# Where k and v of a batch are kept, and when k^T v and the sums of w_in are made, in a one-core attention and feed-forward kernel

## The chip, the cores and the metric

The kernel runs on one core of one Trainium2 chip. The metric is the device time of one execution in microseconds (us); lower is better. One execution was also taken by the hardware profiler, and all readings of engines, waits and transfers come from that one.

## The reference

A linear attention without softmax is followed by a normalisation, and its result goes through a feed-forward block whose activation is a squared ReLU with a scale and a bias. All is float32 in the kernel (weights may come in as wider words and are converted on the chip).

```
# q, k, v: (8 batches, 8 heads, 576 positions, 64); w_in: (512, 2048); w_out: (2048, 512)
kv  = einsum('bhsd,bhse->bhde', k, v)
out = einsum('bhsd,bhde->bhse', q, kv)
out = out / sqrt(mean(out*out, axis=-1) + 1e-6) * g_norm
x   = out.transpose(0, 2, 1, 3).reshape(4608, 512)
h   = x @ w_in
r   = maximum(h, 0)
y   = (s * (r * r) + b) @ w_out
```

## The kernel before, in words

**Chunks and units.** The 4608 rows of x are cut into 36 chunks of 128 rows, and four chunks make a unit: nine units, u = 0 to 8. Unit by unit the kernel multiplies 512 rows by w_in (the part called mm1), squares, and multiplies by w_out (mm2), while the attention of the next unit's four chunks is worked in between. Unit 0 also converts the weights and forms the sums of blocks of w_out, and works its first product plainly.

**Fewer products by sums.** From unit 1 on the products use Strassen's scheme in the variant of Winograd: seven products of half-size blocks instead of eight, with sums of blocks of both operands. For mm1 the names x1, x6, y7, x5, x3, y4 are steps of one of four slices s of w_in's columns; slices come in pairs (d = 0: slices 0 and 1, d = 1: slices 2 and 3), and in the code a is the first slice of the pair and b the second. One of the seven products is itself made by a second level of the scheme, for both slices of a pair together: `mm1_twice`, m[1], m[2], m[6], m[7], m[5], m[34]. The sums of w_in's blocks that these need are made once, by VectorE in unit 1: `sums_w_in(s)` (lines 245 to 259: four operations of 128x512 for a slice) and `sums_w12(s)` (lines 267 to 273: four operations of 128x128 for a slice). `sums_w(s, *more)` (line 1274) calls both.

**The steps that matter here.** m[1] adds its product from PSUM into the hidden tile by an addition on VectorE (`to`, line 663, shown as L231 in the profile, since `add` is a helper), and m[6] accumulates into the bank that this addition has read. Step x6 ends with a copy of its PSUM bank into a tile r2 by ScalarE (ACT; `keep`, line 606). r2 has one buffer, so b's r2 is written only when a's has been read, by the addition in y4 (line 644). x5 accumulates into the bank that r2 was copied from.

**k^T v.** `kv_product(b)` makes, for a batch, the 64x64 product of every head, on quarters of TensorE's array, into two PSUM tiles, and ACT copies them into the block-diagonal bd_kv. Batches 0 and 1 are made in unit 0. Batches 2 to 7 fall due in units 1 to 6 (`kv_due`, line 1238), and are made in two halves of four heads (`kv_half`, line 1280): the first after a["x6"] of d = 0, the second after a["x3"] of d = 1. Both halves come through one buffer of their own (`late["kv"]`, line 1107), so a half is loaded when the half before it has been multiplied: four DMAs of 288 KB for a half, two of k and two of v. The very first of them is issued when unit 0 is done (line 1357).

**The ring of w_out's operands.** The blocks of w_out and their sums lie in DRAM and come in through seven buffers of 128x1024 floats (`ringp`, line 1103). `queue_w2` (line 709) is the list of all these loads in the order of their use, and `pump(k)` issues the next k of them. Unit 0 ends with pump(7), and mm2 calls pump(2) after every other step or so, so that seven loads stay ahead.

**The queues.** The order of each engine's work is that of the code[...]. All loads and stores of this part are issued by SyncE (SP), in the code's order: out's stores, the ring's loads, k and v, and q. `loads(u, i)` (line 1240) loads q of the next unit's chunks in two parts: i = 0 at the unit's start, i = 1 after the place of the first kv half. VectorE turns q (line 418): the first two chunks of the next unit at `second["turns"]` in d = 1, the other two during mm2.

Of the kernel before, what the change touches and what calls it, by code (L numbers as in the profile page):

```python
# [9 lines left out]
FP32 = mybir.dt.float32  # L10
# [6 lines left out]
def kernel(  # L17
# [40 lines left out]
    nc = tc.nc  # L58
    P = 128
    B, H, S, D = q.shape  # L60
    DM = H * D
    DF = moe_w_in.shape[1]
    HB = P // 2
    R = S // HB
    JC = S // 32
    NP = H // 2
# [4 lines left out]
    U = CH // 4  # L71
    NS = FC // 4
    HN = DM // 2
# [10 lines left out]
    ps_t = ctx.enter_context(tc.tile_pool(name="ps_t", bufs=2, space=bass.MemoryType.PSUM))  # L84
# [10 lines left out]
    kv_in, q_in, w_raw = {}, {}, {}  # L95

    def load_kv(b, i, pool, queues=(nc.sync, nc.sync), **kw):

        t = pool.tile([P, 4 * R * D], U32, name="kv_sb", **kw)
        kv_in[b, i] = t.bitcast(FP32).rearrange("p (m l j d) -> p m l j d", m=2, l=2, j=R)  # L100
        for m, src in enumerate((k, v)):
            for r, queue in enumerate(queues):
                h = NP * r + 2 * i
                queue.dma_start(  # L104
                    out=kv_in[b, i][r * HB : r * HB + HB, m].rearrange("p l j d -> p l (j d)"),
                    in_=src[b, h : h + 2].rearrange("h (p j) d -> p h (j d)", j=R),
                )

    def parts(c):
# [229 lines left out]
    for h in range(H):  # L339
        e = D // KC  # L340
        nc.gpsimd.dma_start(
            out=g_col[h * e : h * e + e, :], in_=g_norm.rearrange("(e c) -> e c", c=KC)
# [19 lines left out]
    def warm(n):  # L362

        ps = ps_f.tile([P, 2, TB], FP32, name="warm_ps", tag="z", bufs=1)
        for _ in range(n):
            matmul(ps[:, 0, :P], ident, ident, True, True)

    kv_ps = {}

    def kv_product(b, halves=(0, 1)):  # L370


        if halves[0] == 0:
            kv_ps[b] = [ps_t.tile([P, 2, D], FP32, name="kv_ps", tag="t") for _ in range(2)]
        ps = kv_ps[b]
        for i in halves:
            if b == 0:
                warm((18, 7)[i])
            kv = kv_in.pop((b, i))
            for j in range(R):  # L380
                for l in range(2):
                    for r in range(2):
                        rows = slice(r * HB, r * HB + HB)
                        nc.tensor.matmul(  # L384
                            ps[r][l * HB : l * HB + HB, i, :],
                            lhsT=kv[rows, 0, l, j, :],
                            rhs=kv[rows, 1, l, j, :],
                            start=(j == 0),
                            stop=(j == R - 1),
                        )  # L390
        if halves[-1] == 0:
            return
        for r in range(2):
            for l in range(2):
                ls = slice(l * HB, l * HB + HB)
                to = bd_kv[b % 2][ls, 2 * r : 2 * r + 2, ls].rearrange("p i (c e) -> p i c e", c=KC)
                src = ps[r][ls].rearrange("p i (e c) -> p i c e", c=KC)
                if b == 0 and l == 1:
                    nc.vector.tensor_copy(out=to, in_=src)
                else:  # L400
                    nc.scalar.copy(to, src)
# [296 lines left out]

    ring = {}
    ORDER = (1, 2, 6, 7, 5, 3, 4)
    late = {}

    def twice(u, i):
        return u > 1 and i in TWICE

    queue_w2 = [
        (u, i, n) for u in range(1, U) for i in ORDER for n in range(4 if twice(u, i) else 2)  # L710
    ]

    def pump(k):

        for u, i, n in queue_w2[:k]:
            t = late["ring"].tile([P, 4 * HN], FP32, name="w2_sb", tag="w2")
            if twice(u, i):
                t = t.rearrange("p (m f n) -> p m f n", m=2, n=P)
                k2 = min(2, 7 - 2 * n)
                nc.sync.dma_start(out=t[:, :k2], in_=w3_dram[i][:, 2 * n : 2 * n + k2])  # L720
            else:
                t = t.rearrange("p (f n) -> p f n", n=HN)
                nc.sync.dma_start(out=t, in_=w2_dram[i][:, 4 * n : 4 * n + 4])
            ring[u, i, n] = t
        del queue_w2[:k]
# [375 lines left out]
    def tc_late():  # L1101
        convp.release()
        late["ring"] = ctx.enter_context(tc.tile_pool(name="ringp", bufs=7, side="right"))
        late["sub"] = ctx.enter_context(tc.tile_pool(name="subp", bufs=5, side="right"))
        late["tmp"] = ctx.enter_context(tc.tile_pool(name="tmpp", bufs=4, side="right"))
        late["w"] = ctx.enter_context(tc.tile_pool(name="latep", bufs=1, side="right"))
        late["kv"] = ctx.enter_context(tc.tile_pool(name="kvp", bufs=1, side="right"))

    blocks = [i for s in range(NS) for i in (2 * s, NU + 2 * s)]
    blocks += [FC + 2 * s for s in range(2 * NS)]  # L1110
# [39 lines left out]
    for i in range(2):  # L1150
        load_kv(0, i, kv0p, two, tag="kv")
# [81 lines left out]
            }  # L1233
        return side

    kv_due = {(b // 2 * R + b % 2 * 4) // 4 - 1: b for b in range(2, B)}

    def loads(u, i):  # L1240
        if u + 1 < U:
            load_q(4 * u + 4 + 2 * i)
# [15 lines left out]
    for u in range(U):  # L1258
        if u > 0:
            loads(u, 0)  # L1260
        steps = [mm1(u, s) for s in range(NS)] if u > 0 else []

        def x3(a):
            for name in ("x3", "x3_square", "x3_s1", "x3_s3"):
                a[name]()

        def y4(a):
            for name in ("y4", "y4_square"):
                a[name]()

        side = side_of(u)
        second = mm2(u, steps[-1], side) if u > 1 else mm2(u)

        def sums_w(s, *more):
            for sums in sums_w_in(s):
                sums()
            for s in more:
                sums_w12(s)

        def kv_half(i):  # L1280
            kv_product(kv_due[u], (i,))
            if i == 0:
                load_kv(kv_due[u], 1, late["kv"], tag="kv")
            elif u + 1 in kv_due:
                load_kv(kv_due[u + 1], 0, late["kv"], tag="kv")

        if u == 0:
            first_unit()
        for d in range(NS // 2 if u > 0 else 0):
            a, b = steps[2 * d : 2 * d + 2]  # L1290
            m = mm1_twice(u, d)
            if u == 1 and d == 0:
                x21_sums(1)
                sums_w(1, 0, 1)
            a["x1"]()
            if d:
                x3(steps[2 * d - 1])
                y4(steps[2 * d - 1])
            b["x1"]()
            m[1]()  # L1300
            a["x6"]()
            if d == 0:
                if u in kv_due:
                    kv_half(0)
                loads(u, 1)
            elif u > 1:
                second["turns"]()
            m[2]()
            m[6]()
            a["y7"]()  # L1310
            m[7]()
            m[5]()
            a["x5"]()
            if d == 0 and u == 1:
                sums_w(2)
            m[34]()
            a["x3"]()
            if d and u in kv_due:
                kv_half(1)
            for name in ("x3_square", "x3_s1", "x3_s3"):  # L1320
                a[name]()
            y4(a)
            if u == 1 and d == 0:
                sums_w(3, 2, 3)
            b["x6"]()
            b["y7"]()
            if d and u > 1:
                second["sums"]()
            b["x5"]()
        if u > 1:  # L1330
            second["rest"]()
            continue
        for n, slot in enumerate(second):
            slot()
            if u == 0:
                if n == 1:
                    for i in range(2):
                        load_kv(1, i, convp, tag="raw", bufs=3)
                    store_w2(1)
                    loads(0, 0)  # L1340
                    loads(0, 1)
                    store_w2(5)
                elif n == 2:
                    t2 = convp.tile([P, 4 * R * D], FP32, name="w_t2", tag="raw", bufs=3)
                    W2_AT[6] = t2[:, : FC // 2 * HN].rearrange("p (f n) -> p f n", n=HN)
                    for i in range(14, 16):
                        more(i)
                    sub_w_out(6, 3, 5)
                    store_w2(3, 2, 6)
            if n == 0 and u > 0:  # L1350
                x3(steps[-1])
                y4(steps[-1])
            for step in side.get(n, []):
                step()
        if u == 0:
            tc_late()
            load_kv(kv_due[1], 0, late["kv"], tag="kv")
            pump(7)


# [28 lines left out]
```

## Time and profile before

| | |
|---|---|
| Median of the runs | 961.72 us (960.79 to 964.14, 3 runs) |
| The profiled execution | 961.81 us, of which 960.0 us is the span from the first instruction to the last |
| Mean granted clock of TensorE | 0.996 of full speed |
| TensorE busy with matmuls | 940.3 us |
| VectorE busy | 641.4 us |
| ScalarE busy | 194.8 us |
| DMA | 151.11 MB moved, mean 157 GB/s |
| k and v loads by SP | 60 DMAs of 288 KB, median 4.3 us (k) and 5.5 us (v) from issue to landing |

PE is TensorE's matmuls, PEld its weight loads, DVE is VectorE, ACT is ScalarE, SPq is SyncE's queue of DMA issues. In the lines that are shown below, a line of the timeline gives the start in us, the time in us, the engine, the line of the code, the operation, what it writes and reads with sizes, how many records are merged, and in brackets how long the engine stood idle before it and for whom. A line of the waits gives who waited for whom, the total, how often, and the longest. A line of a stretch gives its limits and length, the busy time of PE, PEld, DVE, ACT and POOL with the number of records, the granted clock, the busy share of the DMA engines, and GB/s. A matmul of float32 is recorded as two instructions: a kv product of 72 matmuls has 144 records.

### The profile page before, as it was taken

The numbers are of one execution on the slowest core, as the hardware profiler recorded it, in microseconds if no ns is written. First come the engines' busy times: TensorE is split into PE (matmuls) and PEld (weight loads), VectorE is DVE, ScalarE is ACT, GpSimd is POOL, SyncE is SP. The second block draws the span as 40 slices with busy tenths as digits, with TensorE's granted clock in tenths as the row PEclk, the third lists the DMA queues.
The fourth block names the chain that finished last, engine by engine and source line by source line (L and its number), as shares of the span: only waits on it lengthen the run. The fifth ranks groups of instructions, "written<-read, shape, count | busy, mean of one in ns | idle before, by whom it ended". The sixth has DMA issues, their size and how long they took to land.

```text
span 960.0 us, 17707 instructions
## 1 busy us (share of the span) xinstructions
PE 940.3 (98%) x7294; PEld 844.4 (88%) x7294; DVE 641.4 (67%) x1212; ACT 194.8 (20%) x366; POOL 6.7 (1%) x18
## 2 busy tenths in 40 slices
PE   7999997999999999999999999999999999999997
PEld 7888886788889998899889998989899989998997
DVE  2789765776566864787468746884678567865673
ACT  3783130111111121102121211111111111121100
POOL 2000000000000000000000000000000000000000
PEclk9999998999999999999999999999999999999999
DMA  9689737368644647255626563556415541642063
GB/s 244 209 304 248 245 84 228 74 196 259 206 111 103 206 147 181 64 177 192 171 36 185 186 181 77 158 183 196 89 54 190 184 103 34 209 153 89 17 224 100
DMA packets 131711, 151.11 MB, mean 157 GB/s; under 512 B 76592, under 2 KB 89136, under 8 KB 131504
## 3 DMA queue, kind: packets, MB, share of 16 engines
q1 hardware_dynamic: 128528, 148.22, 53.3%
q10 hardware_dynamic: 2784, 1.77, 0.8%
q8 instruction: 57, 0.93, 0.4%
q14 instruction: 22, 0.18, 0.1%
q0 software_dynamic: 320, 0.00, 0.0%
HBM read 125.83 MB, written 24.12 MB: 156 GB/s over the span
## 4 chain that ended last, share of the span: by engine, by line
PE 94%; DMA 3%; DVE 2%; ACT 1%; SPq 0%; issue 0%; ACTq 0%; DVEq 0%
PE x_ps L92 48%; PE y_ps L92 31%; PE z_ps L92 9%; PE x_ps L448 3%; PE kv_ps L384 2%; DMA w_raw<-in_moe_w_in_dram 1%; DMA kv_sb<-in_k_dram 1%; DMA kv_sb<-in_v_dram 1%; SPq L104 0%; PE qT_ps L427 0%; DVE xn L467 0%; DVE xT L491 0%; DVE a L231 0%; DVE a L561 0%; ACT xT L497 0%
## 5 line engine op out<-in xcount | busy, mean ns | idle before, releaser
L92 PE MATMUL x_ps<-w_sb,a 128*128 128x256 f32 (+1 forms) x600 | 130.9, 371 | 0.0
L92 PE MATMUL x_ps<-xs,ws 128*128 128x256 f32 x512 | 121.1, 379 | 2.1 <-ACT r L606 2.1
L92 PEld LDWEIGHTS x_ps<-w_sb,a 128*128 128x128 f32 x600 | 108.6, 190 | 15.1 <-issue 1.6
L92 PE MATMUL y_ps<-xs,wb 128*128 128x256 f32 x512 | 121.8, 381 | 0.0
L92 PEld LDWEIGHTS x_ps<-xs,ws 128*128 128x128 f32 x512 | 94.7, 190 | 14.0 <-ACT r L606 2.5
L92 PEld LDWEIGHTS y_ps<-xs,wb 128*128 128x128 f32 x512 | 95.3, 191 | 12.2
L231 DVE TENSOR_TENSOR a<-a,z_ps 128x256 f32<-128x256 f32 x112 | 45.6, 419 | 88.9 <-PE z_ps L92 65.1
L92 PE MATMUL y_ps<-w_sb,sub 128*128 128x128 f32 x728 | 89.3, 275 | 0.0
L92 PE MATMUL x_ps<-xT,wa 128*128 128x256 f32 x384 | 88.3, 380 | 0.1
L92 PEld LDWEIGHTS y_ps<-w_sb,sub 128*128 128x128 f32 x728 | 86.8, 192 | 1.3 <-DVE r L746 0.2
L231 DVE TENSOR_TENSOR a<-y_ps,r 128x512 f32<-128x512 f32 x64 | 44.1, 688 | 63.2 <-ACT r L606 58.3
L92 PEld LDWEIGHTS x_ps<-xT,wa 128*128 128x128 f32 x384 | 72.3, 190 | 10.2 <-ACT xT L497 0.5
L606 ACT COPY r<-x_ps 128x512 f32<-128x512 f32 x64 | 37.5, 586 | 209.8 <-PE x_ps L92 172.7
L92 PE MATMUL y_ps<-w_sb,a 128*128 128x128 f32 (+1 forms) x472 | 70.0, 294 | 0.0
L92 PEld LDWEIGHTS y_ps<-w_sb,a 128*128 128x128 f32 x472 | 63.7, 191 | 4.1 <-issue 1.4
L561 DVE SCALAR_TENSOR_TENSOR a<-a 128x512 f32<-128x512 f32 (+1 forms) x80 | 63.8, 798 | 2.5
L92 PE MATMUL x_ps<-xT,ws 128*128 128x256 f32 x256 | 61.7, 384 | 0.0
L92 PE MATMUL x_ps<-w_sb,s 128*128 128x256 f32 x256 | 59.1, 384 | 0.0
L92 PEld LDWEIGHTS x_ps<-w_sb,s 128*128 128x128 f32 x256 | 47.4, 190 | 8.4 <-issue 2.6
L92 PEld LDWEIGHTS x_ps<-xT,ws 128*128 128x128 f32 x256 | 46.8, 190 | 5.7
L457 ACT ACTIVATE xn<-x_ps 128x512 f32<-128x512 f32 x34 | 20.3, 597 | 148.0 <-PE x_ps L448 146.6
L234 DVE TENSOR_TENSOR a<-a,a 128x512 f32<-128x512 f32 x72 | 48.0, 686 | 0.9
(137 smaller groups left out, 1162.8 us busy)
## 6 DMA issues: line engine op xcount, KB each, us to landing
w_sb<-w SPq DMA_DIRECT2D x140, 512.0 KB, 4.6
kv_sb<-in_k_dram SPq DMA_DIRECT2D x30, 288.0 KB, 4.3
kv_sb<-in_v_dram SPq DMA_DIRECT2D x30, 288.0 KB, 5.5
w_raw<-in_moe_w_in_dram SPq DMA_DIRECT2D x8, 1024.0 KB, 7.3
w_raw<-in_moe_w_out_dram SPq DMA_DIRECT2D x8, 1024.0 KB, 5.3
w_sb<-w SPq DMA_DIRECT2D x28, 256.0 KB, 2.8
out_dram<-o SPq DMA_DIRECT2D x104, 64.0 KB, 1.7
q_sb<-in_q_dram SPq DMA_DIRECT2D x144, 32.0 KB, 2.2
```

Source lines behind the costliest of these rows:

```text
L92: nc.tensor.matmul(o, lhsT=lhsT, rhs=rhs, start=start, stop=stop, skip_group_check=True)
L231: nc.vector.tensor_tensor(out=o, in0=a, in1=b, op=ALU.add)
L234: nc.vector.tensor_tensor(out=o, in0=a, in1=b, op=ALU.subtract)
L384: nc.tensor.matmul(ps[r][l * HB : l * HB + HB, i, :], lhsT=kv[rows, 0, l, j, :], rhs=kv[rows, 1, l, j, :], start=(j == 0), stop=(j == R - 1),)
L448: nc.tensor.matmul(ps[32 * p : 32 * p + 32, w, :], lhsT=st["qT"][:, p, 32 * w : 32 * w + 32], rhs=bd_kv[(b if w < 2 else b1) % 2][:, p, :] ...
L457: nc.scalar.activation(st["xn"], st["x"], AF.Square)
L561: nc.vector.scalar_tensor_tensor(t, t, 0.0, t, ALU.max, ALU.mult)
L606: nc.scalar.copy(st[name], src)
```

## The change

k and v of a batch no longer have a buffer of their own. They come through the ring of w_out's operands: four tiles a batch, each with one head of either half (n and NP + n), loaded by `load_kv_into` with four DMAs of 144 KB. The ring's tiles grow to 128x1152 floats. In the queue of loads they stand ahead of the unit's blocks of w_out, so pump brings them in during the unit before (for unit 1, right after unit 0).

The product of a batch is made in one piece, in d = 0 after b["y7"] and before b["x5"]. After it pump(4) refills the four buffers, and then comes the second part of q's loads, in every unit, which stood after a["x6"] before.

In unit 1, sums_w(2) is moved from after a["x5"] to after y4(a), and sums_w(3, 2, 3) from after y4(a) to after b["x5"].

```diff
+    def load_kv_into(t, b, n):
+        kv_in[b, n] = t.rearrange("p (m j d) -> p m j d", m=2, j=R)
+        for m, src in enumerate((k, v)):
+            for r in range(2):
+                nc.sync.dma_start(
+                    out=kv_in[b, n][r * HB : r * HB + HB, m],
+                    in_=src[b, NP * r + n].rearrange("(p j) d -> p j d", j=R),
+                )
...
-    def kv_product(b, halves=(0, 1)):
-        if halves[0] == 0:
-            kv_ps[b] = [ps_t.tile([P, 2, D], FP32, name="kv_ps", tag="t") for _ in range(2)]
-        ps = kv_ps[b]
-        for i in halves:
+    def kv_product(b):
+        ps = [ps_t.tile([P, 2, D], FP32, name="kv_ps", tag="t") for _ in range(2)]
+        for i in range(2):
             if b == 0:
                 warm((18, 7)[i])
-            kv = kv_in.pop((b, i))
+            kv = [kv_in.pop((b, 2 * i + l)) for l in range(2)]
...
-                            lhsT=kv[rows, 0, l, j, :],
-                            rhs=kv[rows, 1, l, j, :],
+                            lhsT=kv[l][rows, 0, j, :],
+                            rhs=kv[l][rows, 1, j, :],
...
-    queue_w2 = [
-        (u, i, n) for u in range(1, U) for i in ORDER for n in range(4 if twice(u, i) else 2)
-    ]
+    queue_w2 = []
+    for u in range(1, U):
+        queue_w2 += [(u, "kv", n) for n in range(NP if u in kv_due else 0)]
+        queue_w2 += [(u, i, n) for i in ORDER for n in range(4 if twice(u, i) else 2)]
     def pump(k):
         for u, i, n in queue_w2[:k]:
-            t = late["ring"].tile([P, 4 * HN], FP32, name="w2_sb", tag="w2")
+            t = late["ring"].tile([P, 2 * R * D], FP32, name="w2_sb", tag="w2")
+            if i == "kv":
+                load_kv_into(t, kv_due[u], n)
+                continue
+            t = t[:, : 4 * HN]
...
-        late["kv"] = ctx.enter_context(tc.tile_pool(name="kvp", bufs=1, side="right"))
...
-        def kv_half(i):
-            kv_product(kv_due[u], (i,))
-            if i == 0:
-                load_kv(kv_due[u], 1, late["kv"], tag="kv")
-            elif u + 1 in kv_due:
-                load_kv(kv_due[u + 1], 0, late["kv"], tag="kv")
...
             a["x6"]()
-            if d == 0:
-                if u in kv_due:
-                    kv_half(0)
-                loads(u, 1)
-            elif u > 1:
+            if d and u > 1:
                 second["turns"]()
...
             a["x5"]()
-            if d == 0 and u == 1:
-                sums_w(2)
             m[34]()
             a["x3"]()
-            if d and u in kv_due:
-                kv_half(1)
             for name in ("x3_square", "x3_s1", "x3_s3"):
                 a[name]()
             y4(a)
             if u == 1 and d == 0:
-                sums_w(3, 2, 3)
+                sums_w(2)
             b["x6"]()
             b["y7"]()
-            if d and u > 1:
+            if d == 0:
+                if u in kv_due:
+                    kv_product(kv_due[u])
+                    pump(NP)
+                loads(u, 1)
+            elif u > 1:
                 second["sums"]()
             b["x5"]()
+            if u == 1 and d == 0:
+                sums_w(3, 2, 3)
...
             tc_late()
-            load_kv(kv_due[1], 0, late["kv"], tag="kv")
             pump(7)
```

More of the change, by code (lines that the diff above doesn't have):

```diff
@@ L99, in load_kv @@
         t = pool.tile([P, 4 * R * D], U32, name="kv_sb", **kw)
-        kv_in[b, i] = t.bitcast(FP32).rearrange("p (m l j d) -> p m l j d", m=2, l=2, j=R)
+        view = t.bitcast(FP32).rearrange("p (m l j d) -> p m l j d", m=2, l=2, j=R)
+        for l in range(2):
+            kv_in[b, 2 * i + l] = view[:, :, l]
         for m, src in enumerate((k, v)):
@@ L104, in load_kv @@
                 queue.dma_start(
-                    out=kv_in[b, i][r * HB : r * HB + HB, m].rearrange("p l j d -> p l (j d)"),
+                    out=view[r * HB : r * HB + HB, m].rearrange("p l j d -> p l (j d)"),
                     in_=src[b, h : h + 2].rearrange("h (p j) d -> p h (j d)", j=R),
+                )
[6 more added lines that the diff above has]
+                    in_=src[b, NP * r + n].rearrange("(p j) d -> p j d", j=R),
                 )
@@ L366, in warm @@
             matmul(ps[:, 0, :P], ident, ident, True, True)
-    kv_ps = {}
-    def kv_product(b, halves=(0, 1)):
-        if halves[0] == 0:
-            kv_ps[b] = [ps_t.tile([P, 2, D], FP32, name="kv_ps", tag="t") for _ in range(2)]
-        ps = kv_ps[b]
-        for i in halves:
+    def kv_product(b):
+        ps = [ps_t.tile([P, 2, D], FP32, name="kv_ps", tag="t") for _ in range(2)]
+        for i in range(2):
             if b == 0:
                 warm((18, 7)[i])
-            kv = kv_in.pop((b, i))
+            kv = [kv_in.pop((b, 2 * i + l)) for l in range(2)]
             for j in range(R):
@@ L390, in kv_product @@
                         )
-        if halves[-1] == 0:
-            return
         for r in range(2):
@@ L697, in mm1_twice @@
         return {1: m1, 2: m2, 6: m6, 7: m7, 5: m5, 34: m34}
+    kv_due = {(b // 2 * R + b % 2 * 4) // 4 - 1: b for b in range(2, B)}
     ring = {}
@@ L1234, in side_of @@
         return side
-    kv_due = {(b // 2 * R + b % 2 * 4) // 4 - 1: b for b in range(2, B)}
     def loads(u, i):
```

## The prediction

> **What bounds the kernel now.** I read the page's busy times and the 40 slices first.
>
> ```profile
> PE 940.3 (98%) x7294; PEld 844.4 (88%) x7294; DVE 641.4 (67%) x1212; ACT 194.8 (20%) x366; POOL 6.7 (1%) x18
> PE   7999997999999999999999999999999999999997
> ```
>
> TensorE sets the time: 98% busy, and the chain puts 94% of the span on it. Only slice 7 (144 to 168 us, in unit 1) falls short in mid-kernel. The waits of TensorE alone name two causes there (two of the four kv waits, 5.6 of the 6.1 us, lie in unit 1; the other 0.5 us is at the start):
>
> ```profile
> engine line waited for: us in total, times, longest us
> PE kv_ps L384 <- DMA kv_sb<-in_v_dram: 6.1, 4, 3.9
> PE x_ps L92 <- ACT r L606: 2.1, 1, 2.1
> ```
>
> What unit 1 loses in all, the timeline of weight loads shows. Products into the hidden layer run from the first load of a["x1"] to the first load after b["x5"] of the second pair, in unit 1 and then in unit 2, which has the same work and no wait:
>
> ```profile
> 141.16 3.43 PEld L92 LDWEIGHTS x_ps<-xT,wa 128*128 128x128 f32 x16
> 198.77 3.43 PEld L92 LDWEIGHTS x_ps<-w_sb,a 128*128 128x128 f32 x16
> 255.84 3.43 PEld L92 LDWEIGHTS x_ps<-xT,wa 128*128 128x128 f32 x16
> 303.05 1.08 PEld L92 LDWEIGHTS x_ps<-w_sb,a 128*128 128x128 f32 x8
> ```
>
> 57.61 us against 47.21: unit 1 loses 10.40 us. The timeline around the first wait:
>
> ```profile
> 149.98 0.41 DVE L231 TENSOR_TENSOR a<-a,z_ps 128x256 f32<-128x256 f32 x1
> 151.12 0.44 PE L384 MATMUL kv_ps<-kv_sb 64*64 64x64 f32 x2 [3.95 <-DMA kv_sb<-in_v_dram]
> 153.19 2.19 PE L384 MATMUL kv_ps<-kv_sb 64*64 64x64 f32 x70 [1.63 <-DMA kv_sb<-in_v_dram]
> ```
>
> The first half of k^T v waits 5.58 us for its transfer (issued from 143.37 on). The top line matters next: it is VectorE's addition of the m[1] product, behind the sums of w_in (145.58 to 149.98), so VectorE was late too, under the cover of the DMA. The second wait:
>
> ```profile
> 163.86 0.68 DVE L231 TENSOR_TENSOR ws<-wb 128x512 f32<-128x512 f32 x1
> 170.37 0.68 DVE L231 TENSOR_TENSOR a<-y_ps,r 128x512 f32<-128x512 f32 x1
> 171.16 0.59 ACT L606 COPY r<-x_ps 128x512 f32<-128x512 f32 x1 [5.99 <-DVE a L231]
> 171.80 1.99 PE L92 MATMUL x_ps<-xs,ws 128*128 128x256 f32 x8 [2.08 <-ACT r L606]
> ```
>
> b["x5"] waits 2.08 us for ACT's copy r2, which waits for y4's addition (it reads the old r2), which stands behind sums_w(2) on VectorE (163.86 to 166.39). The rest, 10.40 - 5.58 - 2.08 = 2.74 us, is mostly a slow clock. Stretches of 1 us:
>
> ```profile
> 150.00:151.00 1.00, 0.00 (x0) 0.00 (x0) 0.40 (x2) 0.00 (x0) 0.00 (x0) 0.85 0.91 239
> 156.00:157.00 1.00, 1.00 (x7) 1.00 (x7) 0.42 (x1) 0.00 (x0) 0.00 (x0) 0.50 1.03 410
> ```
>
> The column after the five engines is the granted clock: half speed from about 150.7 to 157.5.
>
> [...]the clock fell some 3.5 us after TensorE ran dry at 147.2, and the 2.08 us wait left it at 1.00. [...]
>
> **The change part by part.**
>
> *kv product in one piece.* A half of 72 matmul records costs the time that it pushes the next product back. Unit 2, second half:
>
> ```profile
> 295.04 1.14 PEld L384 LDWEIGHTS kv_ps<-kv_sb 64*64 64x64 f32 x72 [0.33 <-issue]
> 296.25 1.59 PEld L92 LDWEIGHTS y_ps<-xs,wb 128*128 128x128 f32 x8
> ```
>
> x3 before it loaded at 293.12, so 3.13 us to the next product, against 1.62 without kv (269.17 to 270.79): 1.51 us. The first half costs 1.51 as well (259.85 to 262.99, against 1.63). Batch 1's whole product, 144 records, pushes the next load from 107.46 to 110.04: 2.58 us. One piece saves 2 x 1.51 - 2.58 = 0.44 us in each of units 1 to 6. The piece has twice as many DMAs to wait for; once they have landed I take this as free, since halves with and without such waits (unit 3's first, without) both show 0.33 and 1.14.
>
> *Unit 1, first wait.* With kv gone from there, m[2] follows a["x6"] at once. Where nothing interferes (second pair), m[6]'s first matmul comes 2.29 us after a["x6"]'s load (180.87 to 183.16): 145.17 + 2.29 = 147.46. But it accumulates into the bank of m[1], and VectorE reads that only at 149.98 to 150.39. VectorE's queue up to there is unchanged and full. With 0.06 us of hand-over (171.75 to 171.80), m[6] starts at 150.45: **a new wait of 2.99 us takes the place of 5.58**. I take the clock as kept, since 2.99 is under the 3.5 that lost it.
>
> *Unit 1, second wait.* sums_w(2) now stands behind y4's addition, and VectorE's queue ahead of r2 is unit 2's, where r2 ends at 275.85 and x5's first matmul comes at 276.18 without waiting. The kv piece ahead of b["x5"] adds 2.58 us of slack. The 2.08 us go.
>
> *Unit 1, what is late next.* sums_w(3, 2, 3), 4.40 us of VectorE (171.69 to 176.09), comes after b["x5"] instead of before its addition. Counted from b["x5"]'s load: addition at 2.81 (275.97 to 278.78), it and relu_sq 1.41 (176.09 to 177.50), the sums 4.40, then x3's three steps, y4's two and the m[1] addition 3.87 (177.91 to 181.78): 12.49. m[6] of the second pair wants it at 11.36 (171.80 to 183.16). With the hand-over a new wait of 1.19 us; it could be 0 to 2.
>
> *Unit 1's sum.* 47.21 - 0.44 + 2.99 + 1.19 = 50.95, against 57.61: 6.66 us less. Units 2 to 6: 5 x 0.44 = 2.20. **Together 8.86 us.**
>
> *What must stay hidden, on SP.* A batch's k and v are 16 DMAs of 144 KB instead of 8 of 288 KB. At 0.63 us each, as those of 288 KB, that is 10 us of SP in the last part of the unit before, past which out's stores and q's first load (q of 4u+4, 4u+5) are moved. In units 3 to 6 q's issue ends some 16.5 us into the unit (3: 357.06 to 373.8) and VectorE turns it 30.2 us in (286.01): cover 11 us, more than the whole 10. Unit 2 has 32 q DMAs, ending at 281.0, 25.2 us in; with 2.2 us to land and the turn 1.1 us later than before (2.58 - 1.51), cover is about 3.8 us. There SP idles at 241.6 to 246.4 while waiting for VectorE, so I expect a slip of 1 to 2. After the product pump(4) waits on TensorE, and behind it stands the second q load: in unit 4 (48 DMAs, 25.3 us) from 21 us + 1.4 for w2, it lands at about 50, needed at 72.5 (328.35 in unit 2). The ring's next pump is due 49.4 us in (305.24). The last kv tile of a unit goes out at about 1.7 to 4.2 us (358.78), lands within the longest 9.4, needed at 18. In unit 1, 2.36 MB instead of 1.18 must come in: the half took 7.6 us from 145.5, so both are there by 161 at worst; needed at about 163.2 (y7 loads at 150.45 + 0.33, b["y7"] 10.37 later as in unit 2, 263.87 to 274.24, then its 1.72 and the drain of 0.33). ACT's four copies (1.08 us) stand in another place with 2 us of slack. Zero for all of these; bounds for the hardest, unit 1's kv: 0 to 2 us of wait; below zero nothing, as nothing waits on SP today.
>
> **Sum.** The profiled execution took 961.81 us (960.0 of span and 1.8 around it): 961.81 - 8.86 = **953.0**. It lies 0.09 above the median of 961.72, so no correction is needed. This measurement can tell 0.3%, 2.9 us, from no change.
>
> **The rivals.**
> - *The clock falls in the 2.99 us wait* (12%): it is near the 3.5. Half speed for 3.4 to 6.8 us costs 1.7 to 3.4: 954.7 to 956.4. [...]
> - *Part of it doesn't come* (20%): unit 1's kv late by 1 to 2, or the second wait only moved (2.08 stays), or one piece not saving its 0.44 six times (2.64): 954 to 956. For it: kv's cover of 2 us is thin. Against: the queue order of unit 2 works today.
> - *q becomes the bound in unit 2* (5%): if SP's slip before q exceeds 3.8 us, VectorE stands at the turn and the m[ ] additions behind it, then TensorE. It eats the gain from a slip of 12.7 and is slower by 0.3% from 15.6. Were each small kv DMA to take 1.1 us (the slowest of before took 1.74), 16 make 17.6, a stall of 13.8: 967. Against: SP's idle stretches absorb some, and 0.63 needs only 10.
> - *As worked out* (60%): 952 to 954.3. The remaining 3% are for a gain that I don't see, 950 to 952.
>
> **How the numbers follow.** 953.0 is the likeliest case. The range, 951.0 to 956.5, takes in the first two rivals and the missing 1.19 us wait. Faster by over 0.3% (under 958.8) 0.93, within it 0.04, slower 0.03 (from the q case).
>
> **What would show it.** In the profile after: no kv wait in unit 1; before m[6] some 3 us of wait on VectorE's addition near 150.4; none on ACT's r2; about 1 us before m[6] of the second pair; the clock at 1.00 throughout; 144 kv records with one 0.33 us drain a unit; units 2 to 6 some 0.4 us shorter. Wrong would be a kv wait on a DMA, VectorE waiting at the q transposes, or half clock near 150.

## The result, and the profile after

The changed kernel takes 957.20 us in the median of 6 runs (955.40 to 957.88); the kernel before, run beside it, takes 962.36 (960.79 to 964.14, 6 runs). The ratio is 0.9943, with a 95% interval of 0.9930 to 0.9957. So the change is faster by some 5.2 us, where 8.9 was forecast, and 957.2 lies above the range of 951.0 to 956.5. The profiled execution of after took 957.88 us with a span of 956.1; 3.9 us less span than before.

The busy times and the 40 slices of after:

```profile
PE 940.1 (98%) x7294; PEld 845.9 (88%) x7294; DVE 641.4 (67%) x1212; ACT 194.6 (20%) x366; POOL 6.7 (1%) x18
PE   7999998999999999999999999999999999999997
```

The gap of slice 7 is shallower, 8 tenths busy where it was 7. The engines have the same work as before (TensorE is busy for 940.1 us against 940.3), so all that was won is idle time of TensorE. Its waits from 140 to 200 us, the stretch in which before waited 5.6 us for kv and 2.1 us for r2:

```profile
engine line waited for: us in total, times, longest us
PE z_ps L92 <- DVE a L243: 3.6, 2, 2.8
```

Both old causes are gone, and the wait that the prediction put in their place is there, twice. On the timeline, from the start of unit 1 to the first load after b["x5"] of the second pair (times in us, as in the lines of before):

```profile
142.64 3.43 PEld L92 LDWEIGHTS x_ps<-xT,wa 128*128 128x128 f32 x16
151.45 0.94 DVE L243 TENSOR_TENSOR a<-a,z_ps 128x256 f32<-128x256 f32 x2
151.92 0.71 PE L92 MATMUL z_ps<-xs,w 128*128 128x128 f32 x4 [2.83 <-DVE a L243]
166.43 2.42 PEld L392 LDWEIGHTS kv_ps<-w_sb 64*64 64x64 f32 x144 [0.33 <-issue]
168.92 1.99 PE L92 MATMUL x_ps<-xs,ws 128*128 128x256 f32 x8
181.21 0.71 PE L92 MATMUL z_ps<-xs,w 128*128 128x128 f32 x4 [0.77 <-DVE a L243]
195.52 0.62 PEld L92 LDWEIGHTS x_ps<-w_sb,a 128*128 128x128 f32 x3
```

m[6] waits 2.83 us for VectorE's addition of the m[1] product; the kv piece starts at 166.43 without a wait for its transfer; b["x5"] follows it without a wait for r2; m[6] of the second pair waits 0.77. From 142.64 to 195.52 are 52.88 us against 57.61 before. The forecast was 50.95, and what is missing is seen in stretches of 1 us (PE, PEld, DVE, ACT, POOL, then the granted clock):

```profile
152.00:153.00 1.00, 1.00 (x7) 0.95 (x8) 0.72 (x2) 0.00 (x0) 0.00 (x0) 0.96 0.79 230
153.00:154.00 1.00, 1.00 (x4) 0.82 (x3) 0.09 (x1) 0.00 (x0) 0.00 (x0) 0.50 0.73 205
156.00:157.00 1.00, 1.00 (x9) 0.97 (x8) 0.04 (x1) 0.00 (x0) 0.00 (x0) 0.83 0.75 240
```

The clock is halved from 152.93 to 156.34: TensorE's columns say fully busy, but the microseconds from 153 to 156 hold 4, 4 and 5 matmul records, where those from 154 to 158 in e8 below, with the clock at 1.00, hold 6 to 9. The same happened at the start, in unit 0, and not in the profile of before:

```profile
23.00:24.00 1.00, 1.00 (x8) 1.00 (x7) 0.69 (x1) 1.00 (x6) 0.00 (x0) 0.61 1.03 375
26.00:27.00 1.00, 1.00 (x32) 0.95 (x28) 0.04 (x1) 0.07 (x1) 0.00 (x0) 0.68 0.35 129
```

Half speed from 23.22 to 26.64. Unit 1 starts at 142.64 instead of 141.16.

From unit 2 on, the same stretch (first load of a["x1"] to first load after b["x5"] of the second pair) took 47.21 us in unit 2 and 47.10 in units 3 to 6; after it is 47.08 and 46.98. The forecast gain of 0.44 a unit is 0.13.

The account of the span: -4.73 in unit 1, -0.63 in units 2 to 6, +1.48 at the start; together -3.88, against 960.0 - 956.1 = 3.9.

### The profile page after: what moved, and what is told of

The parts are those of the page before. It is cut to its first block, busy times and chain, and to the rows that moved or that the text cites. A ratio compares the mean times of both kernels' runs of the same rounds, so it can differ in the third digit from the quotient of the medians.

```text
span 956.1 us, 17817 instructions
## 1 busy us (share of the span) xinstructions
PE 940.1 (98%) x7294; PEld 845.9 (88%) x7294; DVE 641.4 (67%) x1212; ACT 194.6 (20%) x366; POOL 6.7 (1%) x18
## 4 chain that ended last, share of the span: by engine, by line
PE 93%; DVE 3%; DMA 2%; ACT 1%; issue 0%; SPq 0%; DVEq 0%; ACTq 0%
PE x_ps L92 48%; PE y_ps L92 31%; PE z_ps L92 8%; PE x_ps L454 3%; PE kv_ps L392 2%; DMA w_raw<-in_moe_w_in_dram 1%; DMA kv_sb<-in_k_dram 1%; DVE ws L246 0%; DVE xs L246 0%; PE qT_ps L433 0%; DVE xT L497 0%; DVE xn L473 0%; DVE a L243 0%; DVE w L246 0%; ACT xT L503 0%
```

## The experiments

The theory after this result: (A) in unit 1 the wait before m[6], which is set by VectorE's queue alone, cost its own 3 us and, through the clock, 1.7 more; (B) the kv piece costs 2.69 us (46.98, less the 44.29 of units 7 and 8, which have no kv) and not the 2.58 of batch 1, since the piece's second half meets its DMA waits in mid-stream. The rivals: to (A), that the 52.88 has its excess in m[6]'s operands or in the transfers; to (B), that one place is worth 0.12 by itself, whatever the waits. "Stretch" below is the one of unit 1 defined above.

**Moving the work that m[6] waits for.** The small sums of w_in (`sums_w12`, for m[ ]) go ahead of the larger `sums_w(1)`, which is put behind m[6]; so that they can be made first, the m[7] block of them gets a place of its own instead of overwriting w_in.

```
e1_w12_first, against after
-        w12[s] = late["w"].tile([P, 3, P], FP32, name=f"w12_{s}")
+        w12[s] = late["w"].tile([P, 4, P], FP32, name=f"w12_{s}")
...
-        sub(w12_at(s, 1, 0), w12_at(s, 0, 0), w12_at(s, 1, 0))
+        sub(w12[s][:, 3], w12_at(s, 0, 0), w12_at(s, 1, 0))
...
-                sums_w(1, 0, 1)
+                sums_w12(0)
+                sums_w12(1)
...
             m[6]()
+            if u == 1 and d == 0:
+                sums_w(1)
```

> The changed kernel, but in unit 1 only the small sums (sums_w12(0), sums_w12(1), 2.0 us of VectorE) stand ahead of a["x1"]; sums_w_in(1) (2.5 us) comes after m[6] (the new block for m[7] gets a place of its own, so that the small sums may come first). Theory, the wait of m[6] costs its own length and the clock: VectorE's addition of m[1] comes 2.5 us earlier, the wait falls from 2.8 to about 0.4 us, the clock does not fall near 150 us, and unit 1's stretch goes from 52.88 to 52.88 - 2.4 - 1.7 = 48.8 us: 4 us less than the changed kernel, some 953 us. Rival, the clock falls in unit 1 for another reason: 50.5 us in the stretch, half speed still there, some 954.8 us. Rival, VectorE is late again behind the moved sums (m[5] or b["x6"] wait): 51 us or more.

Measured: 952.88 us (951.81 to 953.48, 6 runs), ratio to before 0.9911 (0.9895 to 0.9926). The stretch is 48.68. The waits of TensorE, and m[6] on the timeline:

```profile
PE z_ps L92 <- DVE a L243: 1.1, 2, 0.8
...
148.92 0.71 PE L92 MATMUL z_ps<-xs,w 128*128 128x128 f32 x4 [0.30 <-DVE a L243]
```

With 2.5 us of wait gone, 4.2 us went from the stretch: the remaining 1.7 is the half clock, which isn't there in unit 1 any more (before the last products ended, it fell in e1 only at the start, at 22.48). VectorE's queue order sets the wait, and neither operands nor transfers do.

**Half of it.** e2_half_wait is e1 with the first part of `sums_w_in(1)` (its s12) left ahead of the small sums.

```
e2_half_wait, against after (places of the small sums as in e1)
-                sums_w(1, 0, 1)
+                s12_1, s34_1 = sums_w_in(1)
+                s12_1()
+                sums_w12(0)
+                sums_w12(1)
...
             m[6]()
+            if u == 1 and d == 0:
+                s34_1()
```

> The changed kernel, but of sums_w_in(1) the two operations of s34 (1.2 us) come after m[6]. The wait of m[6] should be about 1.6 us instead of 2.8. Theory, [...]no half speed near 150 us, stretch of unit 1 52.88 - 1.2 - 1.7 = 50.0 us. Rival, any wait of over a microsecond there loses it: 51.7 us, with half speed of 3.4 us.

Measured: 954.43 us (953.07 to 955.21, 4 runs), ratio 0.9927 (0.9909 to 0.9946); stretch 50.01. The clock is full from 6.1 us until the last products have ended, at 948 us.

```profile
PE z_ps L92 <- DVE a L243: 2.4, 2, 1.6
```

Here a wait of 1.6 us costs its own length and no more: 50.01 less e1's 48.68 is 1.33, and its wait is 1.33 us longer than e1's 0.30.

**More of it.** e3_long_wait has sums_w(2) ahead as well.

```
e3_long_wait, against after
-                sums_w(1, 0, 1)
+                sums_w(1)
+                sums_w(2, 0, 1)
...
             y4(a)
-            if u == 1 and d == 0:
-                sums_w(2)
```

> The changed kernel, but sums_w(2) (2.5 us) stands ahead of a["x1"] in unit 1 too, so m[6] waits 2.8 + 2.5 = 5.3 us. Theory, [...]half speed from about 151 us on, for one or two steps of 3.4 us, and the stretch of unit 1 grows from 52.88 by 2.5 and by 0 to 1.7: 55.4 to 57.1 us. Rival, the clock has nothing to do with the wait: 55.4 with no half speed, or half speed elsewhere.

Measured: 959.22 us (one run), stretch 55.94. The wait, and two stretches of 1 us:

```profile
PE z_ps L92 <- DVE a L243: 6.1, 2, 5.4
...
150.00:151.00 1.00, 0.00 (x0) 0.00 (x0) 0.96 (x4) 0.00 (x0) 0.00 (x0) 0.65 0.73 187
156.00:157.00 1.00, 1.00 (x3) 0.79 (x3) 0.00 (x0) 0.00 (x0) 0.00 (x0) 0.50 1.00 205
```

The half clock begins at 150.30, before TensorE is released, and holds 6.83 us: twice the 3.41 us of after.

**The start.** e8_warm_start puts eight more dummy products between the first two chunks' transposes of unit 0, to see whether they keep the clock there.

```
e8_warm_start, against after
     turn_x[0]()
+    warm(8)
     turn_x[1]()
```

> The changed kernel with eight more dummy matmuls between the two transposes of xn at the start, where TensorE stands idle from 20.4 to 22.4 us. In the profile of the changed kernel the clock was at half speed from 23.2 to 26.6 us, which the profile of the kernel before did not have, and unit 1 began 1.48 us later. Theory, [...]with the gap filled the clock stays at 1.00 there in every run, the runs lie closer together and their median is 0 to 1.4 us lower, about 956.3. Rival, it has another cause: half speed stays, or the dummies delay xT by up to 0.5 us and the time is the same or higher.

Measured: 958.23 us (956.29 to 960.52, 22 runs), ratio 0.9970 (0.9960 to 0.9979). For the start it is a miss: in the profiled execution the clock is at full speed from 5.1 to 954 us, yet unit 1 begins at 144.14, later than with the half speed of after. Of this, 2.40 us is a pause inside a product of unit 0 that none of the other ten profiles has; what TensorE waited for isn't shown, nor how the dummies bring it about:

```profile
115.28 1.46 PE L92 MATMUL x_ps<-w_t,a 128*128 128x256 f32 x6 [2.40 <-issue]
```

But in unit 1 it shows what the profile of after could not: the same order and the same wait with the clock kept.

```profile
153.41 0.71 PE L92 MATMUL z_ps<-xs,w 128*128 128x128 f32 x4 [2.83 <-DVE a L243]
...
154.00:155.00 1.00, 1.00 (x7) 0.90 (x6) 0.42 (x1) 0.00 (x0) 0.00 (x0) 1.00 0.78 207
```

Its stretch is 51.21, so the half clock cost 52.88 - 51.21 = 1.67 us in after. Over all runs the clock did not always hold. Nine of the 22 have a mean granted clock of 0.999, which leaves no room for 3.41 us at half speed, and a median of 956.98 us; ten have 0.996 or 0.997, which needs such a stretch, and a median of 958.67, 1.69 us more (three, at 0.998, can be either). For the runs without a profile it isn't on record where the clock fell, nor so whether the start kept it in every run, as was expected.

**The kv part alone.** e5_old_sums is after with the sums of w_in where they were before.

```
e5_old_sums, against after
             a["x5"]()
+            if d == 0 and u == 1:
+                sums_w(2)
...
-                sums_w(2)
+                sums_w(3, 2, 3)
...
             b["x5"]()
-            if u == 1 and d == 0:
-                sums_w(3, 2, 3)
```

> The changed kernel with the sums of w_in in their old places (sums_w(2) after a["x5"], sums_w(3, 2, 3) after y4(a)), so the kv part of the change alone. Theory, the kv piece of 2.7 us ahead of b["x5"] covers what r2 waited for: r2's copy ends 2.5 us later, at 168.5 in the time of the changed kernel's profile, x5 starts at 168.9: no wait, and the wait of 0.8 us of m[6] in the second pair goes as well. Stretch of unit 1 52.88 - 0.8 = 52.1 us; the reorder is worth nothing here. Rival, as the prediction has it, the reorder is what takes the 2.08 us away: the stretch is 54 us or more.

Measured: 955.49 us (954.42 to 956.58, 6 runs), ratio 0.9943 (0.9926 to 0.9961); stretch 51.66. The waits from 140 to 200 us, and the second place on the timeline:

```profile
PE z_ps L92 <- DVE a L243: 2.8, 1, 2.8
...
164.56 2.42 PEld L392 LDWEIGHTS kv_ps<-w_sb 64*64 64x64 f32 x144 [0.33 <-issue]
166.07 0.58 ACT L612 COPY r<-x_ps 128x512 f32<-128x512 f32 x1 [5.99 <-DVE a L243]
167.05 1.13 PE L92 MATMUL x_ps<-xs,ws 128*128 128x256 f32 x4
```

ACT's copy r2 is as late as ever, 5.99 us behind VectorE, but it ends at 166.65 and b["x5"] starts at 167.05, behind the kv piece, without waiting. The kv piece alone takes the r2 wait away. And the second pair's m[6] doesn't wait here: its wait in after comes from sums_w(3, 2, 3) in its new place. The stretch of after is 1.2 us longer, 1.0 of it by this wait as the weight loads have it. In the times of the two kernels (same ratio) 1.2 us is below what the intervals can tell.

**The sums alone.** e6_sums_alone is before with the two new places of the sums.

```
e6_sums_alone, against before
             a["x5"]()
-            if d == 0 and u == 1:
-                sums_w(2)
...
-                sums_w(3, 2, 3)
+                sums_w(2)
...
             b["x5"]()
+            if u == 1 and d == 0:
+                sums_w(3, 2, 3)
```

> The kernel before with only the sums in their new places. Theory: the 2.08 us wait of x5 goes, since y4's addition no longer stands behind sums_w(2); the second pair's m[6] then waits about 0.8 to 1.2 us, and the waits for k and v and the slow clock stay. Stretch of unit 1 57.61 - 2.08 + 1.0 = 56.5 us, 1 us less in all. Rival: the 2.08 us turn wholly into the wait of m[6], 57.6 us and no change.

Measured: 959.70 us (957.72 to 961.96, 22 runs), ratio 0.9986 (0.9977 to 0.9995); stretch 56.15. Waits from 140 to 200 us:

```profile
PE kv_ps L384 <- DMA kv_sb<-in_v_dram: 4.7, 2, 3.4
PE z_ps L92 <- DVE a L231: 0.8, 1, 0.8
```

In the kernel before, whose kv halves stood elsewhere, the new order did remove the r2 wait. It is worth 1.3 us there in the medians, which fits the waits: 2.1 won and 0.8 given back at m[6]. The two parts of the change therefore don't add up: both remove the same wait.

**Two pieces from the ring.** e4_two_pieces keeps the ring and splits the product again, after b["x6"] and after b["y7"].

```
e4_two_pieces, against after (kv_product takes its halves as it did in the kernel before)
...
             b["x6"]()
+            if d == 0 and u in kv_due:
+                kv_product(kv_due[u], (0,))
             b["y7"]()
...
-                    kv_product(kv_due[u])
+                    kv_product(kv_due[u], (1,))
```

> The changed kernel, but with the kv product in two halves again, one after b["x6"] and one after b["y7"], both from the ring. Units 3 to 6 spend 46.98 us in their products into the hidden layer in one piece and 47.10 in the kernel before. Theory, [...]two halves give 47.10 again, 0.12 us more per unit, 0.7 us in all. Rival, tiles of the ring are slower to multiply than the old buffer: halves give more than 47.10. Rival of the prediction, one piece is worth 0.44: 47.4.

Measured: 957.06 us (one run). Units 3 to 6 have 47.10 us each, as before the change. Two pieces cost 47.10 - 44.29 = 2.81 us wherever they come from, and one piece 2.69.

**The piece's waits at its head.** e7_waits_head turns the loops over halves and positions round, so that the first matmuls with all four of the batch's tiles, and with them all waits for transfers, stand among the piece's first eight.

```
e7_waits_head, against after (batches 2 to 7; the loop over l and r is in group())
-        for i in range(2):
-            for j in range(R):
+            for j in range(R):
+                for i in range(2):
+                    group(i, j, j == 0 and i == 0)
```

> The changed kernel with the loops of the kv product turned inside out for the batches from the ring: j outside, then the two pairs of heads, so that all four tiles are waited for in the first eight matmuls of the 72 and none in the middle. Same 72 matmuls. Theory, waits in the middle of the piece cost 0.2 us: units 3 to 6 spend 46.78 instead of 46.98 us, 1.2 us less in all six units. Rival, it is the number of waits wherever they stand: 46.98 again. Rival, two groups that alternate in a bank cost more: above 47.

Measured: 955.24 us (952.90 to 956.57, 6 runs), ratio 0.9939 (0.9921 to 0.9957). Weight loads of unit 3, of after and then of e7:

```profile
372.71 2.42 PEld L392 LDWEIGHTS kv_ps<-w_sb 64*64 64x64 f32 x144 [0.33 <-issue]
375.20 1.59 PEld L92 LDWEIGHTS x_ps<-xs,ws 128*128 128x128 f32 x8
```

```profile
370.46 2.19 PEld L390 LDWEIGHTS kv_ps<-w_sb 64*64 64x64 f32 x144 [0.33 <-issue]
372.71 0.30 PEld L92 LDWEIGHTS x_ps<-xs,ws 128*128 128x128 f32 x2
```

The transfers have landed long before, in both, yet the same 144 records take 2.42 us when the last two tiles are first read in the middle and 2.19 when all four are first read at the head; units 3, 5 and 6 fall from 46.98 to 46.75. The loss of after lies almost wholly in the loads right behind the 72nd, the first to read those two tiles (0.2 us more there than in e7). The old order of the loops doesn't show it elsewhere: e4's halves have that order and their waits at their heads, and batch 1 in the kernel before has it too, in one piece from the old larger tiles, and takes 2.21. So the cause is most likely the four matmuls' waits; that it is the waits themselves is argued and not shown. In the time of the whole kernel the 1.2 us of six units don't stand out (0.9939 against 0.9943). Unit 4 is an exception, at 47.55: TensorE pauses ahead of the last three records of its piece (0.49 us by the matmuls, 0.63 by the loads), e9 does so at the same place, and the trace doesn't show what releases it.

**All together.** e9_all joins e1 and e7, and splits the sums that delay the second pair: those of slice 3 go ahead of b["x5"], the small ones stay behind it.

```
e9_all, against after (besides the edits of e1 and e7)
+            if u == 1 and d == 0:
+                sums_w(3)
             b["x5"]()
             if u == 1 and d == 0:
-                sums_w(3, 2, 3)
+                sums_w12(2)
+                sums_w12(3)
```

> What the runs point to, together: the changed kernel with the small sums first and sums_w_in(1) after m[6], sums_w_in(3) moved ahead of b["x5"] with only sums_w12(2) and sums_w12(3) behind it, and the kv product with all its waits in its first eight matmuls. Theory: unit 1's stretch is 48.68 - 0.8 (the second pair's m[6] no longer waits) - 0.23 (kv) = 47.65 us, units 3 to 6 spend 46.75 us, no half speed after the start; some 2 us less than with the small sums first alone, about 951 us. Rival: sums_w_in(3) ahead of b["x5"] makes VectorE's addition for x5 late, and the second pair waits as before: 48.5 us in the stretch, 951.8 us.

Measured: 950.19 us (949.95 to 950.60, 4 runs), ratio 0.9872 (0.9848 to 0.9897); stretch 47.42, units 3, 5 and 6 at 46.75 and unit 4 at 47.53. Its waits of TensorE on VectorE's additions:

```profile
PE z_ps L92 <- DVE a L243: 0.3, 1, 0.3
```

Unit 1 has come to within 0.7 us of the units without waits, and the clock stays full after the start, until the last products have ended. This version beats both kernels.

**Where a wait meets the clock.** The profiles also show that the length of a wait alone does not tell whether the clock falls: the same 2.83 us was followed by half speed in after and by full speed in e8. In each of the eleven profiles the changes of the granted clock, counted from the first record of full speed (4.5 to 7.4 us into the span), come after whole multiples of 3.413 us. In after the clock is full from 6.16, half from 23.22 (5 steps on), full from 26.64, half from 152.93 (43 steps on) and full from 156.34; in before it is full from 7.35, half from 150.71 (42 steps on) and full from 157.53 (44). Cut into steps of this length, the wait of 2.83 us looks different in after (first line) and in e8 (the two others):

```profile
149.52:152.93 3.41, 1.01 (x7) 0.96 (x8) 2.96 (x12) 0.00 (x0) 0.00 (x0) 1.00 0.77 223
148.46:151.87 3.41, 2.13 (x12) 1.74 (x10) 3.34 (x9) 0.71 (x2) 0.00 (x0) 1.00 0.77 229
151.87:155.29 3.42, 1.88 (x11) 1.73 (x12) 2.30 (x9) 0.00 (x0) 0.00 (x0) 1.00 0.77 228
```

In after one step has TensorE without a matmul for 3.41 - 1.01 = 2.40 us, and half speed begins at its end. In e8 the edge of a step cuts the wait into 1.28 and 1.54 us, and the clock stays. The same count for all profiled executions (wait before m[6] of the first pair; in before and e6, for k and v):

| profile | wait of TensorE (us) | most time without a matmul in one step (us) | half speed that followed (us) |
|---|---|---|---|
| e1, e9 | 0.3 | under 0.8 | none |
| e8 | 2.8 | 1.54 | none |
| e2 | 1.6 | 1.63 | none |
| e4, after, e5, e7 | 2.8 | 2.28, 2.40, 2.48, 2.51 | 3.41 |
| e3 | 5.4 | 3.03 | 6.83 |
| e6 | 4.7, in two parts | 3.11 | 6.83 |
| before | 5.6, in two parts | 3.41 | 6.83 |

The start fits in: a step with 1.81 us without a matmul left the clock alone in before (21.00 to 24.41), steps with 1.90 in e1 (19.06 to 22.48) and 2.24 in after (19.81 to 23.22) halved it. From the first full speed on, the steps of the eleven profiles fall into two groups: at full speed, each with 1.81 us or less without a matmul was followed by full speed, and each with 1.90 or more by half speed. Half speed went on for a second step where the first slow step had itself 0.79 to 2.33 us without a matmul (e6, before, e3; 2.03 in before), and ended after one where it had 0.34 or less (0.00 in both of after). The ends of matmuls are modelled in a profile, so these figures are no more exact than they are; and they are a count over eleven profiles, no run having moved a wait against the steps on purpose.

## Why the prediction was wrong in its size

Held against the working of the prediction, in spans, where 8.86 us were forecast and 3.88 came:

| step | forecast | profile of after | missing |
|---|---|---|---|
| waits before m[6] in unit 1 (weight loads) | 2.99 + 1.19 | 3.0 + 1.0 | -0.18 |
| clock in unit 1 | 0 | 1.67 | 1.67 |
| one piece, unit 1 (taken as unit 2's 47.21 - 47.08) | -0.44 | -0.13 | 0.31 |
| one piece, units 2 to 6 | -2.20 | -0.63 | 1.57 |
| start of unit 1 | 0 | 1.48 | 1.48 |
| not itemised | | | 0.13 |
| sum | | | 4.98 |

**Right.** The wait for kv went, a wait of 2.8 to 3.0 us before m[6] took its place (2.99 forecast), the wait for r2 went, the weight loads of a unit stand still for 0.33 us ahead of a 64x64 block (the prediction's drain) once, as at 372.71 in after, where they did twice, and the second pair's m[6] waits (0.77 by the matmuls, 1.19 forecast). The cover on SP held: in unit 1 the kv DMAs are issued from 144.8 to 156.1 and wanted at 166.43, and in no unit does TensorE wait for q. So the side and the waits were forecast; the clock and the size were not.

**The step "I take the clock as kept, since 2.99 is under the 3.5 that lost it" failed.** It was the rival with 12%, and one of the signs that the prediction names for being wrong. The half clock followed this wait in 4 of 5 profiled executions and cost 1.67 us, the lower end of the 1.7 to 3.4 that the rival gave. The 3.5 was the author's estimate from a single fall. In before TensorE ran dry at 147.17, close to the edge of a step at 147.29, and the fall came at the next edge, 150.71. In the table above, half speed followed where one step of 3.413 us held 2.28 us or more without a matmul (2.40 in after), and did not where it held 1.63 or less, as in e8, where an edge cuts the wait near its middle, into 1.28 and 1.54. The first record of full speed, from which the steps are counted, comes at 4.5 to 7.4 us in these profiles. If all positions of the wait against the steps are taken as equally likely, which no run shows, 0.8 to 1.0 us out of every 3.41 us of positions leave no step with more than 1.81 or 1.90 us of it: an estimate of one execution in four that keeps the clock. Of the five profiles one did.

**The term "one piece saves 2 x 1.51 - 2.58 = 0.44" was mis-sized**: 0.12 in units 3 to 6, and this is all that units 2 to 6 missed. Two errors add up to the difference.

- The cost of a half was read at the next product's first load. In the product that follows, the second load comes 108 ns after the first (375.197 and 375.305 us in after), and the next ones 216 ns apart, so 0.108 us of each block is caught up. Two halves cost 2.81 by the end of the unit, not 3.02, and one piece 2.58 - 0.11 = 2.47. The right difference would have been 0.34.
- "The piece has twice as many DMAs to wait for; once they have landed I take this as free": not free in mid-stream. e7 gives the price of having them there, 0.23 us a piece. 2.47 + 0.23 = 2.70, against the measured 2.69. The halves that were called on to prove it free had their waits at the head, where the loads show no price: 0.33 and 1.14 us with and without.

**The start.** Half speed in unit 0 (1.48 us) was not in the prediction. It is in 2 of 11 profiled executions, after and e1, which begin unit 1 at 142.64 and 142.16; the eight others, e8 apart, begin it at 140.70 to 141.16. TensorE's two waits just before it are no longer in after than in before (0.85 and 1.75 us against 0.85 and 1.82). What differs is how much of the time without a matmul falls into one step (2.24 us in after, 1.81 in before), so it is put down to the execution rather than to the change, and part of what the profile of after misses isn't in all the other runs. That agrees with the times. Three of the six runs of after, the profiled one among them, have a mean clock of 0.996 and take 957.5 to 957.9 us; one has 0.999, with no room for a half-speed stretch of 3.41 us, and takes 955.4. The median gained 5.2 where the profile gained 3.9.

**Together.** The clock in unit 1 and the pieces (one of the cases in the rival with 20%) bring 953.0 to some 956.5, the edge of the range; the start brings the profiled execution to some 958 (957.88).

**The step that credits the new order of the sums with the 2.08 us was wrong in its cause**, though its sum was right: in e5 the old order has no r2 wait either, since the kv piece ahead of b["x5"] already outlasts the copy. The prediction had this slack of 2.58 in the same paragraph and didn't draw the conclusion that the reorder was then left with its cost alone, 1.2 us in the stretch.

## What to carry to other kernels

When one wait of the bottleneck engine is taken away, read the queue of the engine that is late next and move its work too: here reordering VectorE's sums (e1) brought the ratio to before from 0.9943 to 0.9911, over half as much again. One observed fall of the clock (in before, 3.5 us after TensorE ran dry) did not tell which waits it follows: look in the profile for the times at which the clock changes, and count the idle time in the steps that they mark off. Here 1.90 us or more without a matmul in a step of 3.413 us was followed by half speed and 1.81 or less was not, so a wait like the 2.83 us of this kernel is priced as its own length plus, by the estimate above, three chances in four of the 1.67 us of a slow stretch. Measure what a block costs to the end of the unit and not to the next instruction, and put all its waits at its head (0.23 us a piece in e7).

## What was not expected of the hardware

- In eleven profiles the granted clock changed only at multiples of 3.413 us, and at full speed 1.90 us or more without a matmul inside one such step was followed by half speed, 1.81 or less was not. The same wait of 2.83 us was followed by 3.41 us at half speed in 4 of 5 executions, and by none in the one where a step's edge cut it into 1.28 and 1.54.
- Matmuls that first read two of the tiles in the middle of a run of 144 small matmul records, long after the transfers had landed, cost 0.23 us: 2.42 us of weight loads, against 2.19 in the run whose first matmuls read all four tiles.
- More dummy products at the start kept the clock at full speed in the profiled execution, and the kernel lost time all the same: 0.9970 (0.9960 to 0.9979) of before, against 0.9943 (0.9930 to 0.9957) for the kernel without them, each held against runs of before on its own chip.
